# Which steps share eight accumulator banks: attention's six-step turn and the down projection's groups

## The chip, the cores and the metric

One Trainium2 core runs one program. TensorE (PE) multiplies; its results go to PSUM, an accumulator memory of eight banks, each 512 float32 values wide on 128 partitions. VectorE (DVE) and ScalarE (ACT) read the banks; GpSimd (POOL) and the DMA queues work on the other memories. The metric is the time of the program on the device in microseconds, the median of several runs.

## The reference, cut to what matters

For 2048 tokens of width 576, a causal attention within four segments of 512 tokens (32 heads of 18) is mixed with a memory of the earlier segments, and the result is gated against a SwiGLU feed-forward of width 4608:

```python
logits = einsum("bhqd,bhkd->bhqk", qs, ks) * scale + mask
a_dot = einsum("bhqk,bhkd->bhqd", softmax(logits), vs)
o = g * (num / den) + (1 - g) * a_dot          # num, den: the memory
a = o @ wo
b = (silu(x @ w_gate) * (x @ w_up)) @ w_down
out = sigmoid((x * gate_w).sum(-1)) * a + (1 - ...) * b
```

## The kernel before, in words

All products are made in float32 accuracy from high and low parts. The program has four stages: projections of q, k and v with the memory (0 to about 235 us), a main stage (to about 1667 us), the last down groups, and the output projection. The change is in the main stage.

**The main stage** runs over `seq`: two halves of the tokens, and in each 36 slices f of the feed-forward's width. A step f makes gate and up of a slice with seven sums of products, `seven(...)` (L985 and L988), into banks 0, 1 and 2, which ScalarE and VectorE copy, add and multiply (L1042 to L1067). After each of the seven comes a `tick()`, which calls `beat(k)`. A beat first runs what `defer` has put off to it (weight splits, loads), then up to `SHARE[k]` = 0, 0, 2, 2, 3, 3, 3, 3 down groups, and between them steps of the attention generator `att_gen`, as a credit allows.

**Down groups.** Every third f, `feed` lists 16 groups: eight blocks of 128 tokens by two parts of the columns (320 and 256). `down_group` makes nine matmuls into one bank (L844: three slices f, three products each), and one VectorE instruction adds the bank to `ya` (L849; L847 copies instead for the first slices). So every third step has a burst of 16 groups, and the two steps after it have none. The bank comes from `group_tile`, banks 3, 4 and 7 in turn. Once attention is done, `c_open` fills `cps`, and groups take `pair_tile`, banks 3 and 4.

**Attention.** A unit (two heads) takes six steps of the generator. Five are `s_bank` (L713): matmuls of q and k into a bank from `ts_tile`; VectorE finds the row minima from it (L719), and in the next step `e_bank` has ScalarE take the exponentials from the same bank (L731), which frees it. `p_bank` then casts (L745, L746) and `x_bank` transposes by DMA (L750). The sixth step is `v_unit` of the unit before (L761, L762): 40 matmuls into a bank from `ts_tile`, which VectorE reduces (L768). `ts_tile` hands out banks 5 and 6 in turn.

The order on every engine is the order in which the code calls the instructions; a tile taken from a bank waits until the readers of the bank's tile before it are done.

```python
    def banks(*ids):
        turn = cycle(ids)
        return lambda shape=(P, L): ps.tile(list(shape), F32, name=f"bank{next(turn)}")
    ...
    half_tile = banks(5, 6)
    pair_tile = banks(3, 4)
    lone_tile = banks(7)
    ...
            t = ts_tile()                       # s_bank, L710
            t = ts_tile([P, 2, 4, 3 * E])       # v_unit, L755
    ...
                for p, q in ((hh, dh), (hh, dl), (hl, dh)):
                    nc.tensor.matmul(t, p, q[:, cs], start=(n == 0), stop=(n == 3 * CH - 1))
```

Other lines that the text names: L118 and L928 are VectorE's subtractions for the low parts of split operands, L232 the one for a block of the weights' rest, which waits for a store of its tile by DMA; L1049 reads and writes banks 0 and 2.

Of the kernel before, what the change touches and what calls it, by code (L numbers as in the profile page):

```python
# [20 lines left out]
P = 128  # L21
# [44 lines left out]
def gated_mix(ctx, tc, xT, xrest, wf, wfr, wfh, wd, wv, wo, beta, cmask, ident, bmask, out):  # L66
# [32 lines left out]
# [3 lines that stand above are left out]
# [3 lines left out]
    pair_tile = banks(3, 4)  # L105
# [4 lines left out]
    a_tile = banks(0)  # L110
    x_tile = banks(1)
    y_tile = banks(2)
    ts_tile = banks(5, 6)
    group_tile = banks(3, 4, 7)

    def split(hi, lo, src):
        nc.scalar.activation(hi, src, AF.Copy)  # L117
# [559 lines left out]
    with ExitStack() as st:  # L677
        cps = []
# [155 lines left out]
        def down_group(c, i, hf, hs, ws, ya, half):  # L834
            b, k = divmod(i, 4)
            cs = (slice(0, 320), slice(320, D))[hf]
            t = (pair_tile if cps else group_tile)([P, 320])[:, :cs.stop - cs.start]
            n = 0
            for f in range(CH * c, CH * c + CH):
                hh, hl = (z[:, b, P * k:P * k + P] for z in hs[half, f])  # L840
                d = ws[half, f]
                dh, dl = d[:, 0], d[:, 1]
                for p, q in ((hh, dh), (hh, dl), (hl, dh)):
                    nc.tensor.matmul(t, p, q[:, cs], start=(n == 0), stop=(n == 3 * CH - 1))  # L844
                    n += 1
            if c == 0:
                nc.vector.tensor_copy(ya[:, i, cs], t)  # L847
            else:
                nc.vector.tensor_add(ya[:, i, cs], t, ya[:, i, cs])  # L849
            if c == FT // CH - 1 and hf and half == 0:  # L850
                stores.append((ffd[i], ya[:, i]))
# [78 lines left out]
        def beat(k=None, half=0):  # L930
            for fn in due.popleft() if due else ():
                fn()
            busy = 1 if groups else 0
            share = 2 if k is None else SHARE[k]
            for n in range(max(share, 1)):
                if groups and n < share:
                    down_group(*groups.pop(0))
                if n % 2 or (not busy and (n or k in QUIET)):
                    continue
                credit[0] += 0.5 if k is None else TICK[half][busy]  # L940
                if credit[0] >= 1:
                    credit[0] -= 1
                    if next(att, att) is att:
                        c_open()
# [150 lines left out]
        def downs(k):  # L1095
            for _ in range(min(k, len(groups))):
                down_group(*groups.pop(0))

        ffs = {n: f_load(n) for n in range(2)}
        for n in range(17):  # L1100
# [6 lines left out]
            if n:  # L1107
                tt = order[n - 1]
                ff = ffs.pop(n - 1)
                for hf in range(2):  # L1110
                    c = slice(288 * hf, 288 * hf + 288)
                    t = chain_tile()
# [67 lines left out]
```

## Time and profile before

| | us |
|---|---|
| median of 3 runs (1762.95 to 1763.73) | 1763.63 |
| the profiled execution | 1765.94 |
| its span, first to last instruction | 1764.2 |
| TensorE busy in it | 1720.6 |
| VectorE busy | 1366.7 |
| ScalarE busy | 1095.4 |

In the profile's rows a time is followed by a length, then engine, line, operation and the tiles written and read; a bracket tells how long the engine sat idle before and what ended that. Groups of rows give the count, the busy time, the mean length in ns and the idle time before with its releasers. Line numbers are those of the kernel before.

### The profile page before, as it was taken

How to read it: one execution, taken by the hardware profiler on the slowest of the kernel's cores; microseconds unless marked ns; L12 is line 12 of the kernel's file. 1: busy time of each engine (PE TensorE's matmuls, PEld its weight loads, DVE VectorE, ACT ScalarE, POOL GpSimd, SP SyncE). 2: the span in 40 equal slices, each digit the busy share in tenths (PEclk: the TensorE clock that was granted, in tenths of full speed). 3: DMA queues.
4: the chain of work that ended last, by engine and by line, in shares of the span. 5: the costliest groups of instructions: out<-in, count | busy, mean ns of one | idle time of the engine just before them, and what ended most of it. 6: DMA issues, size and time to landing. Idle time of an engine off the chain costs nothing.

```text
span 1764.2 us, 34937 instructions
## 1 busy us (share of the span) xinstructions
PE 1720.6 (98%) x11868; PEld 1490.4 (84%) x11868; DVE 1366.7 (77%) x3239; ACT 1095.4 (62%) x2201; POOL 933.7 (53%) x1194
## 2 busy tenths in 40 slices
PE   9999999999999999999998999999999999999999
PEld 7898978788888888887887888888888888888899
DVE  6566578888898888888888677788788777887655
ACT  7665575775676577566656756665766576556511
POOL 4434545566565655655556455555555555555221
PEclk9999999999999999999999999999999999999999
DMA  8653489898998988898979976876777677756534
GB/s 283 222 188 117 164 287 192 209 223 178 220 221 197 186 190 205 174 203 186 202 163 250 280 163 137 187 169 160 160 175 169 150 165 180 169 129 150 166 129 141
DMA packets 524003, 328.06 MB, mean 186 GB/s; under 512 B 411184, under 2 KB 460336, under 8 KB 523824
## 3 DMA queue, kind: packets, MB, share of 16 engines
q1 hardware_dynamic: 523824, 325.83, 75.3%
q8 instruction: 93, 1.52, 0.4%
q14 instruction: 86, 0.70, 0.1%
HBM read 165.76 MB, written 76.09 MB: 137 GB/s over the span
## 4 chain that ended last, share of the span: by engine, by line
PE 76%; ACT 11%; DVE 4%; DMA 3%; issue 3%; POOL 2%; SPq 1%; DVEq 0%; ACTq 0%; POOLq 0%
PE bank L985 27%; PE bank L844 25%; PE bank L140 10%; PE bank L988 4%; PE bank L713 3%; PE bank L761 2%; ACT L1059 2%; ACT pe L731 1%; ACT L978 1%; PE bank L762 1%; PE bank L399 1%; ACT row L1059 1%; DMA pt<-p 1%; ACT bank L1042 1%; PE bank L445 1%
## 5 line engine op out<-in xcount | busy, mean ns | idle before, releaser
L746 POOL TENSOR_TENSOR p<-pe,p 128x512 f16<-128x512 f32 x320 | 374.3, 1170 | 474.7 <-DVE p L745 447.6
L844 PE MATMUL bank<-dw,hh 128*128 128x320 f32 (+1 forms) x2304 | 492.4, 306 | 3.0 <-ACT hh L117 2.9
L844 PEld LDWEIGHTS bank<-dw,hh 128*128 128x128 f32 x2304 | 384.4, 191 | 14.1 <-ACT hh L117 3.1
L731 ACT ACTIVATE pe<-bank,mb 128x512 f32<-128x512 f32 (+3 forms) x512 | 246.1, 522 | 227.3 <-DVE mb L719 224.5
L844 PE MATMUL bank<-dw,hl 128*128 128x320 f32 (+1 forms) x1152 | 342.1, 297 | 0.0
L719 DVE CUSTOM_DVE_ANT_0 scr<-bank,cm 128x512 bf16<-128x512 f32 (+3 forms) x512 | 246.1, 481 | 7.3 <-PE bank L713 0.6
L849 DVE TENSOR_TENSOR ya<-bank,ya 128x320 f32<-128x320 f32 x352 | 158.1, 453 | 82.8 <-PE bank L844 81.9
L844 PEld LDWEIGHTS bank<-dw,hl 128*128 128x128 f32 x1152 | 219.5, 191 | 0.2 <-DVE hl L118 0.2
L988 PE MATMUL bank<-xr,rh 128*128 128x512 f32 x504 | 196.6, 390 | 0.0
L739 POOL TENSOR_SCALAR_AFFINE_SELECT pe<-pe 128x256 f32<-128x256 f32 (+1 forms) x320 | 150.2, 470 | 31.4 <-ACT pe L731 25.9
L745 DVE CAST p<-pe 128x512 f16<-128x512 f32 x320 | 144.3, 451 | 1.4 <-DMA pt<-p 1.4
L713 PE MATMUL bank<-kst,qst 108*128 108x512 bf16 (+3 forms) x512 | 125.2, 306 | 13.3 <-ACT pe L731 13.2
L245 POOL TENSOR_TENSOR ws<-raw 128x256 f32<-128x256 f32 x140 | 120.9, 864 | 18.3 <-DVE wo__22862 L252 4.1
L988 PEld LDWEIGHTS bank<-xr,rh 128*128 128x128 f32 x504 | 94.7, 188 | 20.5
L928 DVE TENSOR_TENSOR hl<-row,hh 128x512 fp32r<-128x512 f32 x120 | 100.9, 841 | 10.7 <-ACT hh L927 10.3
L1052 ACT ACTIVATE row<-bank 128x512 f32<-128x512 f32 x72 | 43.1, 599 | 100.3 <-PE bank L988 100.2
L1057 DVE TENSOR_TENSOR row<-bank,row 128x512 f32<-128x512 f32 x72 | 49.6, 689 | 59.0 <-ACT bank L1056 58.8
L1059 ACT ACT_TABLE_LOAD x72 | 92.4, 1283 | 1.3
L978 ACT ACT_TABLE_LOAD x72 | 92.4, 1283 | 1.0
L761 PE MATMUL bank<-v,pt 128*128 128x57 bf16 x1280 | 77.6, 188 | 12.0 <-ACT pe L731 10.9
L713 PEld LDWEIGHTS <-qst 108*128 108x128 bf16 x512 | 35.8, 98 | 63.1 <-issue 47.0
L140 PE MATMUL bank<-xo,qhi 128*128 128x512 f32 x264 | 83.1, 396 | 0.0
(2165 smaller groups left out, 4114.0 us busy)
## 6 DMA issues: line engine op xcount, KB each, us to landing
raw<-in_wf_dram SPq DMA_DIRECT2D x140, 256.0 KB
rh<-rc SPq DMA_DIRECT2D x72, 336.0 KB
dc<-dw SPq DMA_DIRECT2D x36, 576.0 KB
dw<-dc SPq DMA_DIRECT2D x36, 576.0 KB
stk<-q SPq DMA_DIRECT2D x32, 384.0 KB
draw<-in_wd_dram SPq DMA_DIRECT2D x36, 288.0 KB
rc<-rt SPq DMA_DIRECT2D x42, 224.0 KB
vd<-vps SPq DMA_DIRECT2D x8, 912.0 KB
```

The lines of the kernel that those rows point to most:

```text
L140: nc.tensor.matmul(t, st[n], mv[n], start=(n == 0), stop=(n == 13))
L713: nc.tensor.matmul(t[:, c:c + w], qs[:KR, pr, P * i:P * i + P], ks[:KR, pr, 0:w], start=True, stop=True)
L719: nc.vector.tensor_tensor_reduce(scr[:, :w], t[:, c:c + w], cm[:, L - w:L], -SCALE, 3.0e38, OP.add, OP.min, m[:, k:k + 1])
L731: nc.scalar.activation(pe[:, c:c + w], t[:, c:c + w], AF.Exp, bias=m[:, k:k + 1], scale=SCALE)
L739: nc.gpsimd.affine_select(d, d, pattern=pat, compare_op=OP.is_ge, fill=0.0, base=0, channel_multiplier=1)
L745: nc.vector.tensor_copy(p[:, 0], pe)
L746: nc.gpsimd.tensor_sub(p[:, 1], pe, p[:, 0])
L844: nc.tensor.matmul(t, p, q[:, cs], start=(n == 0), stop=(n == 3 * CH - 1))
L849: nc.vector.tensor_add(ya[:, i, cs], t, ya[:, i, cs])
L985: nc.tensor.matmul(t, w[:, p, z], x[z][:, q], start=first and n == 0, stop=False, skip_group_check=True)
L988: nc.tensor.matmul(t, rem[:, RPOS[j]], XR[j], start=False, stop=True, skip_group_check=True)
L1059: nc.scalar.activation(sg0, sg0, AF.Silu)
```

## The change

`ts_tile` hands out banks 5, 6 and 7 in turn, so the six steps of a unit go twice round three banks. `group_tile` is gone: down groups take `pair_tile`, banks 3 and 4, in the main stage as well. The number and order of the instructions stay the same on every engine; only the banks and what each first write to a bank waits for differ.

```diff
-    ts_tile = banks(5, 6)
-    group_tile = banks(3, 4, 7)
+    ts_tile = banks(5, 6, 7)
...
-            t = (pair_tile if cps else group_tile)([P, 320])[:, :cs.stop - cs.start]
+            t = pair_tile([P, 320])[:, :cs.stop - cs.start]
```

## The prediction

> **What bounds the kernel now.** I read the page first: the busy shares, then its groups.
>
> ```profile
> span 1764.2 us, 34937 instructions
> PE 1720.6 (98%) x11868; PEld 1490.4 (84%) x11868; DVE 1366.7 (77%) x3239; ACT 1095.4 (62%) x2201; POOL 933.7 (53%) x1194
> ...
> L844 PE MATMUL bank<-dw,hh 128*128 128x320 f32 (+1 forms) x2304 | 492.4, 306 | 3.0 <-ACT hh L117 2.9
> ...
> L849 DVE TENSOR_TENSOR ya<-bank,ya 128x320 f32<-128x320 f32 x352 | 158.1, 453 | 82.8 <-PE bank L844 81.9
> ...
> L713 PE MATMUL bank<-kst,qst 108*128 108x512 bf16 (+3 forms) x512 | 125.2, 306 | 13.3 <-ACT pe L731 13.2
> ...
> L761 PE MATMUL bank<-v,pt 128*128 128x57 bf16 x1280 | 77.6, 188 | 12.0 <-ACT pe L731 10.9
> ```
>
> TensorE (PE) is busy 98% and no other engine is near it, so a microsecond that PE stops waiting is a microsecond of the span, unless PE stops again soon after. The two attention lines wait 13.2 + 10.9 = 24.1 us for ScalarE's exponentials (L731): the step two places earlier has not left its bank. The down groups (L844), with three banks, wait for no VectorE addition (L849) among the releasers shown. The change trades one for the other.
>
> The view of waits gives the counts, the windows view the load of the engines in one 60 us period of each half (three values of f: one burst of 16 down groups, then attention alone beside gate and up):
>
> ```profile
> PE bank L713 <- ACT pe L731: 13.2, 19, 1.2
> ...
> PE bank L761 <- ACT pe L731: 10.9, 8, 4.1
> ```
> ```profile
> 460.00:521.00 61.00, 60.16 (x436) 50.86 (x435) 54.03 (x128) 41.47 (x84) 38.16 (x52) 1.00 0.92 205
> ...
> 1377.00:1437.00 60.00, 59.07 (x433) 50.81 (x432) 46.80 (x117) 37.41 (x75) 33.79 (x45) 1.00 0.73 172
> ```
>
> Columns after the length: busy PE, PEld, DVE, ACT, POOL, clock, DMA. VectorE is at 54.03/61 = 89% in the first half and 46.80/60 = 78% in the second: in the first half it also splits the down weights. It lags most there, and its lag decides what two banks cost.
>
> **Part 1: attention gets a third bank.** An idle gap in the view is shorter than the loss, since a matmul's modelled 0.39 us covers two places of PE's order. From the first burst that I use below:
>
> ```profile
> 459.40 0.69 DVE L118 TENSOR_TENSOR hl<-row,hh 128x512 fp32r<-128x512 f32 x1 [1.79 <-ACT hh L117]
> ...
> 465.65 0.48 DVE L849 TENSOR_TENSOR ya<-bank,ya 128x320 f32<-128x320 f32 x1
> ...
> 472.85 0.62 DVE L232 TENSOR_TENSOR rt<-rr,rt 128x448 fp32r<-128x448 f32 x1 [1.68 <-DMA rc<-rt]
> 473.39 0.48 DVE L849 TENSOR_TENSOR ya<-bank,ya 128x320 f32<-128x320 f32 x1
> ```
> ```profile
> 462.48 0.38 PE L713 MATMUL bank<-kst,qst 108*128 108x128 bf16 x2 [0.47 <-ACT pe L731]
> ...
> 465.14 0.39 PE L988 MATMUL bank<-xr,rh 128*128 128x512 f32 x1
> 465.37 0.45 PE L844 MATMUL bank<-dw,hh 128*128 128x320 f32 x2
> ...
> 472.23 0.46 PE L844 MATMUL bank<-dw,hh 128*128 128x320 f32 x2
> ```
>
> L988 lasts 0.39 but its successor starts 0.23 after it, so each wait costs 0.16 beyond its gap: 24.1 + 27 x 0.16 = 28.4 us. With three banks the step waits for the one three places back, which at every one of these waits had left its bank 2.4 us before or more; so all 28.4 is removed from these instructions. By their start times in the timeline 12 of the waits stand at the opening of a first-half burst (one each, 14.4 us in all), 8 at openings in the second half (7.1 us), and 7 elsewhere (6.9 us).
>
> **Part 2: down groups on two banks.** A group is nine matmuls into one bank, emptied by one addition. Its first matmul will wait for the addition two groups back instead of three. No instruction is added; only waits move. VectorE takes its queue in order, so an addition is late by whatever stands before it.
>
> In the burst above VectorE works without a gap from 459.40 until after the first addition, which ends at 465.65 + 0.48 = 466.13. The third group starts at 465.37; it would have to wait until 466.13 + 0.05 (the distance from a release to PE's start that the waiting rows show), 0.81 late. VectorE's run starts from ScalarE's output at 459.40, before PE's wait at 462.48, so taking away that wait (0.47 + 0.16 = 0.63) doesn't bring the addition forward: PE only arrives earlier and waits longer, and ends 0.81 later than now. The seventh group (472.23) then needs the fifth's addition, which ends at 473.39 + 0.48 = 473.87 and hangs on a DMA (L232), not on PE: 473.92 - 472.23 = 1.69 late. The larger of the two holds, not their sum: this burst ends 1.69 us later than now. The last burst of this form:
>
> ```profile
> 595.04 0.48 DVE L849 TENSOR_TENSOR ya<-bank,ya 128x320 f32<-128x320 f32 x1
> ```
> ```profile
> 594.30 0.46 PE L844 MATMUL bank<-dw,hh 128*128 128x320 f32 x2
> ```
>
> 595.52 + 0.05 - 594.30 = 1.27. The four bursts of this form (starting 399, 460, 522, 583) give 1.27, 1.69, 1.28, 1.27 by this subtraction, 5.5 us; their thirteenth and sixteenth groups add some 0.2 each (estimate): **+6.3**.
>
> The next form (645, 706, 768), the middle one shown:
>
> ```profile
> 703.47 0.69 DVE L118 TENSOR_TENSOR hl<-row,hh 128x512 fp32r<-128x512 f32 x1 [1.43 <-ACT hh L117]
> ...
> 710.31 0.48 DVE L849 TENSOR_TENSOR ya<-bank,ya 128x320 f32<-128x320 f32 x1
> ```
> ```profile
> 704.21 0.38 PE L713 MATMUL bank<-kst,qst 108*128 108x512 bf16 x1 [0.85 <-ACT pe L731]
> ...
> 710.26 0.45 PE L844 MATMUL bank<-dw,hh 128*128 128x320 f32 x2
> ```
>
> Again VectorE runs unbroken from before PE's wait to the addition: 710.84 - 710.26 = 0.58 late, and the 1.01 us gained is lost in the same place. Three times 0.58 and some 0.1 each for later groups: **+2.0**.
>
> Of the other first-half bursts, 276, 339, 831 and 892 have room, but less than the gain:
>
> ```profile
> 895.43 0.48 DVE L849 TENSOR_TENSOR ya<-bank,ya 128x320 f32<-128x320 f32 x1
> ```
> ```profile
> 889.66 0.19 PE L761 MATMUL bank<-v,pt 128*128 128x57 bf16 x1 [1.80 <-ACT pe L731]
> ...
> 896.66 0.45 PE L844 MATMUL bank<-dw,hh 128*128 128x320 f32 x2
> ```
>
> 896.66 - 895.96 = 0.70 of room, so 0.70 of 1.96 is kept. With the same subtraction at the others (room 0.7 at 831, 0.2 at 276 and 339) and a later group 0.76 late at 276, the four come to **-0.5**.
>
> The burst at 953, after the longest wait:
>
> ```profile
> 957.96 0.81 DVE L849 TENSOR_TENSOR ya<-bank,ya 128x320 f32<-128x320 f32 x2
> ```
> ```profile
> 951.92 0.21 PE L761 MATMUL bank<-v,pt 128*128 128x57 bf16 x1 [4.09 <-ACT pe L731]
> ...
> 953.53 0.88 PE L844 MATMUL bank<-dw,hh 128*128 128x320 f32 x2
> ...
> 957.66 0.46 PE L844 MATMUL bank<-dw,hh 128*128 128x320 f32 x2
> ```
>
> The two additions end at about 958.4 and 958.8; the third group starts at 957.66, so it is some 0.8 late, a later one 1.06: **+1.1**, and the 4 us move to the third group. After the wait two matmuls take 0.88 us instead of 0.46: PE is at half rate after such an idle stretch. Since the idle stretch moves and stays as long, I leave that loss as it is. The Trainium skill (TensorE: Matmul & The Clock Gate, Part 1) says that about 3.4 us of idle halves the clock; these rows agree with 4.09 us before the slow ones. By it the shorter waits of 1 to 2 us that I forecast cost nothing more.
>
> Second half, VectorE less loaded:
>
> ```profile
> 1080.70 0.48 DVE L849 TENSOR_TENSOR ya<-bank,ya 128x320 f32<-128x320 f32 x1
> ```
> ```profile
> 1075.60 0.38 PE L713 MATMUL bank<-kst,qst 108*128 108x256 bf16 x2 [0.74 <-ACT pe L731]
> ...
> 1082.60 0.45 PE L844 MATMUL bank<-dw,hh 128*128 128x320 f32 x2
> ```
>
> Room 1082.60 - 1081.23 = 1.37 against 0.90 gained: all kept. Over the half, 7.1 gained less 1.4 in bursts with less room or a late later group: **-5.7**.
>
> The waits elsewhere, first and last of the 7:
>
> ```profile
> 324.69 0.19 PE L761 MATMUL bank<-v,pt 128*128 128x57 bf16 x1 [1.00 <-ACT pe L731]
> ...
> 940.49 0.38 PE L713 MATMUL bank<-kst,qst 108*128 108x128 bf16 x2 [1.15 <-ACT pe L731]
> ...
> 942.32 0.46 PE L985 MATMUL bank<-xo,wo__12871 128*128 128x512 f32 x1
> ```
> ```profile
> 941.53 0.69 DVE L1049 TENSOR_TENSOR bank<-bank,row 128x512 f32<-128x512 f32 x1
> ```
>
> No down group follows these for 9 us or more, so I count them, except where the next PE step is itself at its limit: L985 at 942.32 needs L1049's bank, free at 942.22, so only 0.1 of 1.31 is kept there, and some 0.2 is lost at a small one. 6.9 - 1.4 = 5.5: **-5.5**.
>
> **Sum:** 6.3 + 2.0 - 0.5 + 1.1 - 5.7 - 5.5 = -2.3 us. The profiled execution took 1765.94 us (1.7 around its span) and the median of the runs is 1763.63, 2.3 below it; I carry the difference over unchanged: 1763.63 - 2.3 = **1761.3**. A measurement of this kernel can tell about 0.2%, 3.5 us; the forecast is no change that can be told.
>
> **Rivals.** *VectorE paces the first half (slower).* Everything there is measured against VectorE at 89%: if it is no earlier when PE is, the 5.5 us of the elsewhere waits return at the next burst, less the 1.1 of the first one, whose burst has no shortfall: 4.4 lost. And if the fifth addition moves back with the stalled PE, the shortfalls add up: 0.81 in each of four bursts, 0.3 in three (estimate), 0.8 at 953: 5.0. Together -2.3 + 9.4 = +7.1: 1770.7. It decides as soon as VectorE has no idle time between a stall and the next shortfall. For it: 89%, and runs of 7 to 10 us without a gap. Against it: the DMA at 472.85, which PE doesn't move, and gaps of 1.4 to 1.8 us that let VectorE follow PE.
>
> *The gains are kept (faster).* If the additions come forward with PE, the shortfalls alone cost, as counted, and most openings keep their gain. Half of the 14.4 us kept gives -2.3 - 7.2: 1754.1. Against it: both unbroken runs above.
>
> *A rule of buffers (much faster).* If a group never waited with two banks, because the addition of one always falls under the next, all 28.4 us would stay: 1735.2. The late additions above speak against it. The Trainium skill (Perfetto Trace Analysis, Matmuls and Optimization Strategy) says that groups should rotate through banks so that emptying one overlaps the next, and that repeated gaps can mean too little PSUM; by it two banks would do for groups, which the 0.81 and 1.69 above contradict.
>
> *Nothing moves*, if PE's wait for the exponential only goes to a later PE instruction for another reason: 1763.6.
>
> **How the numbers follow.** Forecast 0.48, of it 0.17 below -3.5 us, 0.30 within, 0.01 above (its own range is 1757 to 1766, from pricing the openings and the later groups either way). VectorE pacing 0.36 (0.33 slower, 0.03 within); gains kept 0.12 (0.11 faster, 0.01 within); the rule 0.02; nothing 0.02. Faster 0.30, same 0.36, slower 0.34. The range runs from the gains-kept case, 1753, to beyond the pacing one, 1773 (its two costs could be a quarter larger); about 0.07 lies below it and 0.09 above.
>
> **What would show it.** Right: no PE wait for L731 at L713 and L761; new PE waits at L844 for L849, some 15 to 25 us in all, mostly in first-half bursts at the third and seventh groups, few after 1018; the first half longer by 1 to 5 us, the second shorter by 5 to 6. Wrong: L844 waits under 10 us or over 30, attention still waiting for exponentials, or a second half that gains nothing.

## The result, and the profile after

The changed kernel takes 1770.58 us (median of 5, 1767.58 to 1772.31) against 1763.63 us (5 runs): ratio 1.004, 95% interval 1.0029 to 1.0051. It is slower by 7 us; the forecast was 1761.3, no change that can be told. The profiled execution of the changed kernel took 1767.58 us, its fastest. The difference between the two numbers is the clock, and comes last in this section.

The page after (lines behind the change have a number one lower: L844 is now L843, and so on):

```profile
span 1765.9 us, 34942 instructions
PE 1725.3 (98%) x11868; PEld 1484.9 (84%) x11868; DVE 1367.3 (77%) x3239; ACT 1096.9 (62%) x2201; POOL 932.6 (53%) x1194
...
L843 PE MATMUL bank<-dw,hh 128*128 128x320 f32 (+1 forms) x2304 | 497.0, 308 | 22.9 <-DVE ya L848 19.1
L843 PEld LDWEIGHTS bank<-dw,hh 128*128 128x128 f32 x2304 | 381.0, 190 | 45.1 <-DVE ya L848 28.5
...
L848 DVE TENSOR_TENSOR ya<-bank,ya 128x320 f32<-128x320 f32 x352 | 158.9, 453 | 89.2 <-PE bank L843 87.8
...
L712 PE MATMUL bank<-kst,qst 108*128 108x512 bf16 (+3 forms) x512 | 125.7, 307 | 0.0
```

Attention's 13.2 us of waits at L712 are 0.0. The down groups, which waited for no addition, now wait 19.1 us for L848, or 28.5 us seen from the weight load that comes before the first matmul. The trade is there as forecast; its price is not.

The burst that the prediction walked through (460 us before), first VectorE, then PE in the changed kernel:

```profile
457.75 0.69 DVE L117 TENSOR_TENSOR hl<-row,hh 128x512 fp32r<-128x512 f32 x1 [1.79 <-ACT hh L116]
...
464.02 0.48 DVE L848 TENSOR_TENSOR ya<-bank,ya 128x320 f32<-128x320 f32 x1
...
471.18 0.62 DVE L231 TENSOR_TENSOR rt<-rr,rt 128x448 fp32r<-128x448 f32 x1 [0.72 <-DMA rc<-rt]
471.73 0.48 DVE L848 TENSOR_TENSOR ya<-bank,ya 128x320 f32<-128x320 f32 x1
```
```profile
459.95 0.39 PE L712 MATMUL bank<-kst,qst 108*128 108x128 bf16 x2
...
462.64 0.39 PE L987 MATMUL bank<-xr,rh 128*128 128x512 f32 x1
464.55 0.56 PE L843 MATMUL bank<-dw,hh 128*128 128x320 f32 x2 [1.52 <-DVE ya L848]
...
472.26 0.56 PE L843 MATMUL bank<-dw,hh 128*128 128x320 f32 x2 [0.58 <-DVE ya L848]
```

The attention step no longer waits, PE reaches the third group early, and stands until the first addition ends at 464.50. The place, the releaser and the 0.05 us after the release are those of the forecast.

To see where the time went I compare the start of the same instruction (L988 before, L987 after; seven in each step, 504 in all) in both traces: the first half is the stretch from the 4th to the 246th, the break from there to the 253rd (the start of the second half), and the second half the rest.

| | first half | break | second half | main stage |
|---|---|---|---|---|
| forecast | +2.3 | +1.1 | -5.7 | -2.3 |
| measured | +6.7 | +2.4 | -3.8 | +5.2 |

Outside these the changed kernel's profiled execution was 1.6 us shorter before the main stage and 1.9 us shorter after it, though not an instruction differs there. The windows view, 0 to 100 and 1667 to 1720 us, before and then after, shows what does (the number after the busy times is the granted clock):

```profile
0.00:100.00 100.00, 95.99 (x514) 82.34 (x515) 63.86 (x136) 71.39 (x146) 44.81 (x55) 0.98 0.73 246
...
1667.00:1720.00 53.00, 50.05 (x361) 49.26 (x360) 28.19 (x56) 10.38 (x24) 13.09 (x16) 0.94 0.47 156
```
```profile
0.00:100.00 100.00, 97.25 (x527) 83.55 (x528) 65.16 (x142) 72.23 (x148) 45.26 (x56) 1.00 0.74 246
...
1667.00:1720.00 53.00, 49.55 (x362) 47.92 (x361) 30.46 (x56) 12.30 (x26) 12.81 (x15) 1.00 0.53 179
```

The profiled execution of before had stretches at half clock there, that of after had none. So the profiled difference, 1.6 us, is the main stage's 5.2 less 3.5 that the clock gave by chance. Over the runs the chance is the other way: by clock (0.993, 0.994, 0.995, 0.996) the mean spans of 15 runs of before are 1764.1, 1763.2, 1761.2 and 1760.2, those of the five of after 1769.8, 1770.5, 1767.8 and 1765.9: 5.7 to 7.3 apart at the same clock.

### The profile page after: what moved, and what is told of

It reads as the page before. It is cut to its first block, busy times and chain, and to the rows that moved or that the text cites. A ratio compares the mean times of both kernels' runs of the same rounds, so it can differ in the third digit from the quotient of the medians.

```text
span 1765.9 us, 34942 instructions
## 1 busy us (share of the span) xinstructions
PE 1725.3 (98%) x11868; PEld 1484.9 (84%) x11868; DVE 1367.3 (77%) x3239; ACT 1096.9 (62%) x2201; POOL 932.6 (53%) x1194
## 3 DMA queue, kind: packets, MB, share of 16 engines
q8 instruction: 93, 1.52, 0.4%
## 4 chain that ended last, share of the span: by engine, by line
PE 75%; ACT 8%; DVE 8%; issue 4%; POOL 2%; DMA 2%; SPq 1%; DVEq 0%; ACTq 0%; POOLq 0%
PE bank L984 28%; PE bank L843 24%; PE bank L139 10%; PE bank L987 5%; PE bank L712 3%; PE bank L760 2%; DVE hl L927 1%; ACT L1058 1%; PE bank L761 1%; DVE scr L718 1%; ACT L977 1%; PE bank L398 1%; POOL ws L244 1%; DVE p L744 1%; ACT pe L730 1%
## 5 line engine op out<-in xcount | busy, mean ns | idle before, releaser
L843 PE MATMUL bank<-dw,hh 128*128 128x320 f32 (+1 forms) x2304 | 497.0, 308 | 22.9 <-DVE ya L848 19.1
L843 PEld LDWEIGHTS bank<-dw,hh 128*128 128x128 f32 x2304 | 381.0, 190 | 45.1 <-DVE ya L848 28.5
L843 PE MATMUL bank<-dw,hl 128*128 128x320 f32 (+1 forms) x1152 | 341.2, 296 | 0.2 <-DVE hl L117 0.2
L848 DVE TENSOR_TENSOR ya<-bank,ya 128x320 f32<-128x320 f32 x352 | 158.9, 453 | 89.2 <-PE bank L843 87.8
L843 PEld LDWEIGHTS bank<-dw,hl 128*128 128x128 f32 x1152 | 218.8, 190 | 0.4 <-DVE hl L117 0.4
L987 PE MATMUL bank<-xr,rh 128*128 128x512 f32 x504 | 196.5, 390 | 0.0
L712 PE MATMUL bank<-kst,qst 108*128 108x512 bf16 (+3 forms) x512 | 125.7, 307 | 0.0
L987 PEld LDWEIGHTS bank<-xr,rh 128*128 128x128 f32 x504 | 94.7, 188 | 20.5
L1056 DVE TENSOR_TENSOR row<-bank,row 128x512 f32<-128x512 f32 x72 | 49.6, 689 | 60.1 <-ACT bank L1055 59.9
L1055 ACT ACTIVATE bank<-bank 128x512 f32<-128x512 f32 x72 | 42.0, 583 | 73.2 <-PE bank L987 72.5
L1041 ACT ACTIVATE bank<-bank 128x512 f32<-128x512 f32 x72 | 41.6, 578 | 66.3 <-PE bank L987 66.3
```

The lines of the kernel that those rows point to most:

```text
L712: nc.tensor.matmul(t[:, c:c + w], qs[:KR, pr, P * i:P * i + P], ks[:KR, pr, 0:w], start=True, stop=True)
L987: nc.tensor.matmul(t, rem[:, RPOS[j]], XR[j], start=False, stop=True, skip_group_check=True)
```

## The experiments

**Theory A:** two banks cost what VectorE's queue makes the additions late, much in the first half, little in the second; attention's third bank gains in both. **Rivals:** B, the third bank gains nothing that lasts; C, the clock; D and F, below. The stretches of all runs against the kernel before, by the same instructions:

| run | first half | break | second half | median, us |
|---|---|---|---|---|
| changed kernel | +6.7 | +2.4 | -3.8 | 1770.58 |
| two and two | +10.7 | +1.5 | +1.8 | 1778.06 |
| second half alone | +0.2 | 0.0 | -0.5 | 1762.99 |
| first half alone | +7.4 | +3.2 | +0.2 | 1772.82 |
| lent | -6.7 | -0.6 | -7.0 | 1747.71 |
| changed, on GpSimd | +4.4 | +3.7 | -4.0 | 1767.22 |
| before, on GpSimd | +2.0 | -0.4 | 0.0 | 1764.17 |
| changed, loaded | +7.9 | +3.6 | +4.1 | 1780.71 |
| before, loaded | +0.5 | +0.1 | +1.7 | 1767.76 |

Each stretch comes from one profiled execution. Where two runs have the same arrangement in a stretch they differ by up to 1.2 us (first half: 6.7, 7.4, 7.9), so differences below that carry nothing. In the two halves the granted clock was full in all these executions but for one stretch at half clock, 3.4 us long, in the second half of "second half alone" (from 979.5 us) and one in the first half of "before, on GpSimd" (from 395.3 us). The kernel before took 1764.27 (15 runs) beside the first four experiments and 1763.96 (23 runs) beside the others.

**Two and two.** Bank 7 stays idle in the main stage.

```diff
-    group_tile = banks(3, 4, 7)
+    group_tile = banks(3, 4)
```

> Down groups on banks 3 and 4, attention on 5 and 6 as before; bank 7 is idle in the main stage. Theory A (in the first half the groups' late additions eat what attention gains, in the second half the gain stays): the first half is slower than the kernel before by about as much as in the changed kernel or up to 4 us more (6.6 there by the start of the step at 935 us), the second half slower by 1 to 2 us instead of 3.7 us faster, the break some 2 us slower: 1772 to 1776. Rival B (attention's third bank gains nothing that lasts; the two banks of the groups cost the 7 us alone): the same time as the changed kernel, 1770, in both halves. Rival C (the 7 us are the clock's half-rate windows, not banks): 1764 to 1767.

Measured: 1778.06, ratio 1.008 (1.0066 to 1.0094), above A's own range. Taking a bank from the groups costs 10.7 us in the first half, where 6.7 remain if attention gets it, and 1.8 in the second, where 3.8 are gained if attention gets it. So the third bank is worth about 4 and 5.6 us to attention, and B falls. C falls too: over both halves the clock was full in the traces of before, of the changed kernel and of this run, so their differences there aren't the clock's.

**One half at a time.** The banks are chosen by the half:

```diff
-    ts_tile = banks(5, 6)
-    group_tile = banks(3, 4, 7)
+    phase = [0]
+    ts_of = banks(5, 6), banks(5, 6, 7)
+    group_of = banks(3, 4, 7), banks(3, 4)
+
+    def ts_tile(*shape):
+        return ts_of[phase[0]](*shape)
...
-            t = (pair_tile if cps else group_tile)([P, 320])[:, :cs.stop - cs.start]
+            t = (pair_tile if cps else group_of[half])([P, 320])[:, :cs.stop - cs.start]
...
+            phase[0] = half
```

The other kernel has the two pairs exchanged.

> The change in the first half and its last burst alone. Theory A: slower by what the first half and the break cost in the changed kernel's trace, 6.6 + 2.4 = 9 us: 1770 to 1774. Rival B: about half of the change's cost, 1766 to 1768. Rival C: within 1 us of the kernel before.

> The change in the second half alone: the first half and its last burst keep two banks for attention and three for groups. Theory A: 3 to 5 us faster than the kernel before (the second half gained 3.7 us in the changed kernel's trace): 1758.5 to 1760.5. Rival B: not faster, 1763 to 1766. Rival C: within 1 us of the kernel before.

Measured: the first half alone 1772.82, ratio 1.0048 (1.0034 to 1.0062), as A expected. The second half alone 1762.99, ratio 0.9997 (0.9988 to 1.0006): no gain that can be told, a miss for A's total. The timeline of that run shows why, at the change of the banks (the first steps of the second half):

```profile
975.50 1.52 PE L989 MATMUL bank<-xo,wo__13123 128*128 128x512 f32 x6
...
979.18 0.38 PE L717 MATMUL bank<-kst,qst 108*128 108x256 bf16 x2 [1.93 <-ACT pe L735]
979.32 2.74 PE L989 MATMUL bank<-xo,wo__13152 128*128 128x512 f32 x6
```

The new turn starts at bank 5, which the step before still held: 1.93 us of wait, and the six matmuls after it take 2.74 instead of 1.52 us, at half clock. The wait and the half clock cost 3.5 us within the first step; from there to the end the half gains 4.0, as in the changed kernel. So the gain per stretch is there, but the change of banks itself ate it.

**Lent.** Attention takes the longest unused of banks 5, 6 and 7, except from the third beat of a burst step until the groups are done, when it has 5 and 6; groups take the longest unused of 3, 4 and 7.

```diff
-    ts_tile = banks(5, 6)
-    group_tile = banks(3, 4, 7)
+    used, clock, tight = {}, [0], [False]
+
+    def oldest(ids, shape=(P, L)):
+        n = min(ids, key=lambda i: used.get(i, 0))
+        clock[0] += 1
+        used[n] = clock[0]
+        return ps.tile(list(shape), F32, name=f"bank{n}")
+
+    def ts_tile(*shape):
+        return oldest((5, 6) if tight[0] else (5, 6, 7), *shape)
+
+    def group_tile(*shape):
+        return oldest((3, 4, 7), *shape)
...
             busy = 1 if groups else 0
+            tight[0] = bool(groups) and (k is None or k > 1)
```

> Bank 7 is lent: attention takes the longest unused of banks 5, 6 and 7 while no down group is about to run (from the first matmuls of a burst step's third part on it has 5 and 6 alone), groups the longest unused of 3, 4 and 7. Theory A: most of attention's 28.4 us of waits stand at the openings and between the bursts and go, while the groups keep their third bank: 8 to 20 us faster, 1744 to 1756. Rival D (the third group of a burst waits for the exponentials that still hold bank 7): 1762 to 1770, with waits at the down groups for L731's line. Rival B: 1763 to 1766.

Measured: 1747.71, ratio 0.9908 (0.9895 to 0.9922), faster than the kernel before by 16.6 us in the medians and faster than the changed kernel. About 2 us of that are the clock's: at equal mean clock (0.994 and 0.996) the runs are 14.4 and 13.9 us apart, and the main stage of the trace is 14.3 us shorter. PE's waits over the main stage (230 to 1667 us) in this run:

```profile
PE bank L772 <- DMA pt<-p: 5.4, 8, 1.5
...
PE bank L855 <- DVE ya L860: 1.7, 1, 1.7
...
PE bank L724 <- ACT pe L742: 1.4, 3, 0.7
...
PE bank L772 <- ACT pe L742: 0.8, 1, 0.8
```

Of 24.1 us for exponentials 2.2 are left, of the 19.1 for additions 1.7. That is A without the price; D (the third group held up by attention's bank) appears only in two waits of a down group (L855) for attention's readers, 0.2 us for L742 and 0.8 us for L779. About half of the 28.4 us becomes time: transposed tiles now come late (L772 for a DMA, 5.4 us), and other steps reach their own limits.

**VectorE lightened.** One subtraction, in the first half part of VectorE's unbroken run ahead of the first addition, goes to GpSimd, in the changed kernel and, as a control, in the kernel before.

```diff
-            split_by(1, d[:, 0], d[:, 1], r)
+            defer(1, lambda: nc.scalar.activation(d[:, 0], r, AF.Copy))
+            defer(2, lambda: nc.gpsimd.tensor_sub(d[:, 1], r, f32(d[:, 0])))
```

> The changed kernel with one subtraction (the low part of the down weights, 36 times 0.75 us, one of them right ahead of each first-half burst's first addition) moved from VectorE to GpSimd. Theory A (the third group waits for a first addition that stands late in VectorE's queue): that addition comes some 0.6 us earlier in each of 11 first-half bursts, so the first half is 4 to 7 us shorter than in the changed kernel (6.65 longer than before there, then 0 to 2.5), the second half unchanged; 1764 to 1767. Rival F (VectorE's load isn't what makes the additions late; ScalarE's output ahead of them is): within 2 us of the changed kernel, 1769 to 1772.

> The same move in the kernel before, as the control. Theory A: PE's waits there are for exponentials, which also come earlier by part of 0.75 us: 0 to 6 us faster, 1758 to 1764, so that less than the whole gain of the run above is owed to the groups if this one gains too. Rival F: 1762 to 1765.

The third group of the burst above in this run:

```profile
464.82 0.39 PE L988 MATMUL bank<-xr,rh 128*128 128x512 f32 x1
466.06 0.56 PE L844 MATMUL bank<-dw,hh 128*128 128x320 f32 x2 [0.85 <-DVE ya L849]
```

Its wait is 0.85 instead of 1.52, shorter by 0.67, what the subtraction took in the queue (458.36 to 459.03 us in the changed kernel). In the eleven bursts the third group is held up less by 0.2 to 0.8 us, 6.2 us in all, as A says. F (ScalarE's output, not VectorE's load) would have left these waits as they were.

The first half is only 2.3 us shorter than in the changed kernel, below the 4 to 7 expected, because the move brings waits of its own. The longest is 1.28 us at 391.12 us, for a bank that ScalarE empties (L1056). The control has it too, and there the half clock follows:

```profile
394.13 1.95 PE L986 MATMUL bank<-xo,wo__4773 128*128 128x512 f32 x6 [1.83 <-ACT bank L1057]
...
396.31 2.67 PE L986 MATMUL bank<-xo,wo__4809 128*128 128x512 f32 x6
```

The half clock costs 1.7 of the control's +2.0. Without it the move costs the control's first half 0.3 us, and against that the change costs 4.1 us there instead of 6.7. In the medians, which come from 11 runs of each, the change costs 3.1 us with the subtraction on GpSimd instead of 7. The median of 1767.22 is just above the expected range. The control, 1764.17, is no faster than before, where A had expected 0 to 6 us and F nothing. So A holds for the groups, but this run doesn't bear out what it said of attention.

**VectorE loaded.** The reverse in the second half: three subtractions of 576 columns in three steps, to an unused tile.

```diff
+                if half and (q, k) in ((1, 4), (1, 7), (2, 7)):
+                    defer(2, lambda g=f - (k == 4): extra(g))
                 beat(k, half)
+
+            def extra(g):
+                d = ds[1, g]
+                r = fp.tile([P, D], F32, name="draw", bufs=1)
+                nc.vector.tensor_sub(r, f32(d[:, 0]), f32(d[:, 1]))
```

> The changed kernel with VectorE's extra load of the first half put into the second too: three subtractions of 576 columns in three steps, at the same places, their output unused. Theory A (the halves differ because VectorE is fuller in the first): the second half's gain of 3.8 us turns into a loss of 0 to 5 us, with waits at the down groups for additions in the second half as in the first: 1774 to 1779. Rival F: the second half keeps 2 to 4 us of gain, 1769 to 1773.

> The same load in the kernel before, as the control. Theory A: attention's waits in the second half grow towards those of the first, 1 to 4 us slower: 1765 to 1768. Rival F: 1763 to 1765.

PE's waits for additions between 1000 and 1667 us, in the loaded changed kernel; in the unloaded one this view has no line of PE at all:

```profile
PE bank L843 <- DVE ya L848: 4.3, 8, 0.8
...
PE bank L843 <- DVE ya L846: 0.8, 1, 0.8
```

The second half turns from -3.8 to +4.1 (control +1.7), its bursts now waiting at the third group as the first half's do: 0.2 to 1.0 us in each of eleven. VectorE is busy there only 49.99/61 = 82% of a period (1387 to 1448 us), less than the 89% of the first half: a smaller load is enough where it stands ahead of the addition. The median of 1780.71, ratio 1.0098 (1.0084 to 1.0112), is above the expected range; the control's 1767.76, ratio 1.0023 (1.0011 to 1.0034), is inside.

## Why the prediction was wrong

**Right:** PE's waits for exponentials went, all of them. They came back as waits of the third group for the first addition, mostly in the first half, and half by half with the signs forecast. The third group's loss, by the subtraction of the prediction (gain at the opening plus shortfall), can be held against the time by which the same matmul is later after than before relative to the group ahead of it. In all eleven bursts of the second half and in six of the first the two agree within 0.03 us (at 706, 1.59 forecast and 1.57 measured; at 892, 1.26 and 1.28). In the other five of the first half the loss was 0.2 to 0.5 us larger (at 460, 1.44 forecast, 1.69 measured).

**Wrong: the sizes of the sum's terms**, each to the same side.

| term | forecast | measured |
|---|---|---|
| four bursts 399 to 583 | +6.3 | +7.3 |
| three bursts 645 to 768 | +2.0 | +3.1 |
| bursts 276, 339, 831, 892 | -0.5 | +0.3 |
| break, burst at 953 | +1.1 | +2.4 |
| second half | -5.7 | -3.8 |
| waits elsewhere | -5.5 | -4.1 |

All signs but that of the third row were right, but together the errors turned a forecast gain of 2.3 us in the main stage into a loss of 5.2. Four steps in the pricing failed.

*A waiting group was priced at its first matmul alone.* The subtraction ends at the release plus 0.05 us. But wherever a group waits, its second matmul is another 0.1 us late: the row of two at 464.55 in the changed kernel lasts 0.56, the one at 465.37 before 0.45. The prediction put nothing for this. It happens at 29 groups of the first half and 14 of the second, 3.1 and 1.5 us: up to 4.5 of the 7.5 us by which the main stage missed the forecast ("up to", because a later wait in the same burst can absorb an earlier one). In the second half, where the gain at the openings was right (7.1 us), it is most of the 1.9 us missed. Why the second matmul is late stays open.

*VectorE's rows were set still, or let follow PE, as each place suggested.* In the burst at 460 VectorE's run starts at 457.75 instead of 459.40, 1.65 earlier; PE, 1.90 earlier before its opening and relieved of its wait there, reaches the third group 2.5 us earlier. VectorE and ScalarE had not gained all that PE had, and the third group gave the difference back. In five first-half bursts that is 1.8 us in all; four of the five follow a wait elsewhere, though two others that follow one lost nothing. This is the pacing rival's first cost, 1.8 us where it asked 4.4. Its second, shortfalls that add up, came in small part: at the seventh group of this burst PE had lost 1.93 us (0.03 later than before, from 1.90 earlier), 0.24 more than the 1.69 of my subtraction, where the rival asked 0.81 more.

*At the waits elsewhere only the next PE step was looked at.* Two more of these gains were given back a few us later by gate and up products that met their own limit: 0.7 us after the wait at 630, and 0.9 after the one at 814, most of it here:

```profile
822.18 1.66 PE L984 MATMUL bank<-xo,wo__11068 128*128 128x512 f32 x6 [0.47 <-DVE bank L1048]
```

Together these make up the 1.4 us missing in the last term.

*"The idle stretch moves and stays as long" did not hold.* At the break most of it did move to the third group, as said, but part of it to a transposed tile before that:

```profile
955.36 0.20 PE L760 MATMUL bank<-v,pt 128*128 128x57 bf16 x1 [1.67 <-DMA pt<-p]
...
959.60 0.43 PE L843 MATMUL bank<-dw,hh 128*128 128x256 f32 x2
959.87 0.28 PE L843 MATMUL bank<-dw,hl 128*128 128x256 f32 x1
963.50 0.90 PE L843 MATMUL bank<-dw,hh 128*128 128x320 f32 x2 [3.35 <-DVE ya L848]
```

The two waits are 1.67 + 3.35 = 5.02 us where 4.09 stood before, 0.9 of the 1.3 us by which this term was too small.

The term of -0.5 for four bursts doesn't follow from its own figures: 0.7, 0.7, 0.2 and 0.2 kept and 0.76 lost give -1.0. And the seventh group at 831, which falls 0.16 short by the same subtraction, wasn't in it; it lost 0.98.

That the pacing rival's 1770.7 is the measured median is luck: its two costs make up less than half of the 7.5 us, and the late second matmuls, which no rival had, up to 4.5. The signs by stretch of the forecast hold; a forecast by stretch of +2.3 and -4.6 that nearly cancel needed each within a microsecond, which rows of one trace did not give.

**The carry to the median** failed too: I moved the profiled difference over unchanged, but the runs differ by how often the clock halves, and at equal clock they are 5.7 to 7.3 us apart, not the 1.6 of the two profiled executions.

**The rule on rotating banks** (the Trainium skill, Perfetto Trace Analysis, Matmuls) was met by both kernels; how many banks a group needs here depends on the queue ahead of the emptying instruction: with the same two banks the third group waits 0.85 or 1.52 us.

## What to carry to other kernels

Before a bank is taken away, look up what stands in the queue ahead of the instruction that empties it, and not only how many waits the other user has. When two users need a scarce buffer at different times, lend it (about 14 us gained here) rather than hand it over (7 us lost). When you price a new wait, follow it one instruction further than its release. And when gain and loss nearly cancel in the sum, the errors of the terms decide the sign; split the test by stage first, and look at the clock of every stretch that you compare, the controls' too.

## What the runs showed of the hardware

Runs of one program spread over 6 us (15 runs of before: spans of 1758.9 us at a mean clock of 0.996 to 1765.2 at 0.993), although the order of work is fixed. In the traces the clock is granted at half in stretches of 3.4 or 6.8 us, most of them around the starts and ends of stages. How long PE had stood idle does not decide it alone. A half-rate stretch began about waits of 1.67 us (955.36 in the changed kernel), 1.83 us (394.13 in the control on GpSimd) and 1.93 us (979.18 with the second half alone). The clock stayed full after waits of 1.80 us (889.66 in the kernel before), 2.15 us (1674.29 in the changed kernel) and 2.98 us (232.75 in the lent kernel). So the prediction's sentence that waits of 1 to 2 us cost nothing more, taken from the Trainium skill's 3.4 us of idle (TensorE: Matmul & The Clock Gate, Part 1), doesn't hold for every place. What else decides, these runs don't show.
